# A gated-recurrence and GELU kernel: products of the identity on TensorE ahead of the first FFN matmul, and a smaller factor on the planned cost of the first attention steps

## The chip, the cores and the metric

One core of one Trainium2 chip (trn2) runs the kernel alone. The metric is the device time of one execution in microseconds; of several executions the median counts. The engines are called PE (TensorE), PEld (its weight loads), DVE (VectorE), ACT (ScalarE), POOL (GpSimd) and SP (SyncE, which issues most of the loads).

## The reference

The first half is a gated linear recurrence for 4 batches of 8 heads, 768 steps, head size 48; the second is a feed-forward layer (FFN) with GELU on its output, 3072 tokens by 384, with 2048 hidden columns. All of it is in float32.

```python
for t in range(S):
    state = alpha[:, :, t, :, None] * state + np.einsum('bhd,bhe->bhde', k[:, :, t], v[:, :, t])
    y[:, :, t] = np.einsum('bhd,bhde->bhe', q[:, :, t], state)
x = np.ascontiguousarray(y.transpose(0, 2, 1, 3)).reshape(B * S, H * D)
h = x @ w_in
g = 0.5 * h * (1.0 + erf(h * inv_sqrt2))
return (g @ w_out).astype(np.float32)
```

## The kernel before

**Attention.** The tokens are cut into 12 groups g of 256 steps. A group has two units (g, u), each four heads. For a unit, DVE makes running products of alpha forwards (`scan`, line 256), multiplies the queries by them (`qv`, line 261), makes them backwards and multiplies the keys (`back`, lines 265 and 268). PE forms the score products and transposes the keys (`scores`, lines 284 and 293) into one PSUM tile s. ACT copies the transposed keys out of it (`kn`, line 300) and DVE multiplies the scores by a mask (`mask`, line 305, output ss). Both read the same tile s, and the build orders them: the mask waits until kn is done. PE then multiplies by the values (`inside`, lines 322 and 340), DVE adds the states of the four chunks (`chain`, lines 357 and 359), PE adds what earlier states contribute (`outer`, line 384), and DVE hands the state on (`carry`, line 364).

**From attention to the FFN.** ACT copies the result as the high part of x (line 426). In the first three groups PE subtracts that part in PSUM (`x_minus`, line 435; its steps are called minus_x0, minus_x1, ...) and ACT copies the rest (line 441). After a group's second unit, small DMAs spread the last rows (line 449).

**FFN.** x and both weights are used as two float32r parts. There are 8 blocks f of 256 hidden columns. A step (g, f) is gemm1 (18 matmuls, line 457), two GELU passes on ACT (ghi and hp, lines 469 and 470), the low part glo (DVE, line 475; in the early steps by PE and ACT, lines 479 and 483), and gemm2 (12 matmuls, line 496) into two accumulators. When the next step belongs to another group, the accumulators are first copied out to a tile part (line 513 on ACT, 511 on DVE).

**Weights.** The 16 pieces of the weights (wi and wo of each f, in turn: piece 0 is wi of f = 0, piece 11 wo of f = 5) come as 64-bit words and are converted on the chip: u on ACT (line 183), c0 and c1 on DVE (lines 187 and 193, giving w), the high part on ACT (line 203: wih, woh), and four more on DVE (lines 206, 215, 224, 234), the last giving the low part (wil, wol). Until all eight f are there, only the first three groups are taken through the FFN.

**What sets the order.** A planner inside the kernel walks through time in steps of 0.05 us with a table of costs, lets each engine take the operation of lowest rank whose predecessors are done, and writes down a start for each. PE, DVE, ACT and SP then get their instructions in the order of these starts; each of them works through its queue in that order. The costs of `scores`, `inside` and `outer` of the first four units are multiplied by SLOW (1.8):

```python
if n < 4:
    for what in ("scores", "inside", "outer"):
        d[what].cost *= SLOW
```

At the very start PE multiplies the identity by itself 22 times (WARM, line 85); a float32 product is two passes on PE. PSUM tiles hp (of gemm1) come from a pool of two buffers.

Of the kernel before, what the change touches and what calls it, by code (L numbers as in the profile page):

```python
# [8 lines left out]
F32 = mybir.dt.float32  # L9
# [14 lines left out]
WARM = 22  # L24
XB = 3
WAIT = 0.15
SLOW = 1.8
UNTIL = 100.0
LANES = 8
RATE, ALONE, LATENCY, SMALL = 400e3, 290e3, 2.1, 50e3  # L30
# [10 lines left out]
def gla_then_gelu_ffn(ctx: ExitStack, tc: tile.TileContext, q, k, v, alpha, akq, w_in, w_out, out):  # L41
    nc = tc.nc
    B, H, D, S = q.shape
    NF, P, NK, _ = w_in.shape
# [3 lines left out]
    G = 2 * C  # L48
# [19 lines left out]
    ps_h = ctx.enter_context(tc.tile_pool(name="ps_h", bufs=2, space=PSUM))  # L68
    ps_o = ctx.enter_context(tc.tile_pool(name="ps_o", bufs=1, space=PSUM))

    ident = const.tile([P, P], F32, name="ident")
# [20 lines left out]
    minus = const.tile([P, P], F32R, name="minus")  # L92
# [551 lines left out]
    def plan_unit(n):  # L644
# [37 lines left out]
# [4 lines that stand above are left out]
# [47 lines left out]
    steps, plan, evacuated = [], [], set()  # L733
# [105 lines left out]
    def choose(e, t):  # L839
        best = None  # L840
        for o in waiting[e]:
            at = when(o)
            if at is not None and at <= t + 1e-9 and (best is None or (o.rank, o.n) < (best.rank, best.n)):
                best = o
        if e != "PE":
            return best
        if best is not None and not (best.late and best.at() + MARGIN > t):
            return best
        held = best
        second = [s for s in steps if s["gemm2"].start is None]  # L850
        if second:
            at = when(second[0]["gemm2"])
            if at is not None and at <= t + 1e-9:
                return second[0]["gemm2"]
        if len(second) < 2:
            hp_free = steps[-2]["low"].end if len(steps) > 1 else 0.0
            if hp_free is not None and hp_free + WAIT <= t + 1e-9 or len(steps) < 2:
                g = next_step(t)
                if g is not None:
                    return gemm1_op(g, t)  # L860
        return held
# [3 lines left out]
    while True:  # L865
        moved = False
        for e in ("DVE", "ACT", "PE", "SP", "POOL"):
            if free_at[e] <= t + 1e-9:
                o = choose(e, t)
# [12 lines left out]
    last["last"] = True  # L882
    plan.append(Op("DVE", "part", lambda: last["out"](), [last["gemm2"]]))
    plan[-1].start = t + 10
    plan.sort(key=lambda o: (o.start, o.n))

    by_hand = ExitStack()
# [71 lines left out]
```

## Time and profile before

| | |
|---|---|
| median of 3 runs | 534.9 us (534.61 to 537.7) |
| profiled execution | 533.34 us |
| its span, first to last instruction | 531.8 us |
| PE busy | 510.3 us (96%) |
| PEld busy | 492.8 us (93%) |
| DVE busy | 284.3 us (53%) |
| ACT busy | 207.8 us (39%) |
| mean granted clock of PE | 0.976 |

The busy shares are means over the span. In the kernel's first 80 us DVE is nearly full and PE isn't; later it is the other way round. A granted clock of 1.00 stands for 2.4 GHz, 0.50 for 1.2 GHz.

### The profile page before, as it was taken

What the parts mean: (1) busy time and instruction counts of PE and PEld (TensorE: products, weight loads), DVE (VectorE), ACT (ScalarE), POOL (GpSimd) and SP (SyncE); (2) the same over time, 40 slices, a digit from 0 to 9 for tenths busy, and PEclk for the clock granted to TensorE, in tenths of its full rate; (3) what the DMA queues carried; (4) which work ended last, traced back from release to release, by engine and by line L of the source; (5) the groups of instructions that cost most, each with busy time, mean ns of one, the idle gap of its engine ahead of it and who ended that gap; (6) DMA issues with size and microseconds to landing.
All of it is one profiled execution on the core that took longest, in us unless ns stands there. A gap on an engine that the chain in (4) does not pass through costs nothing.

```text
span 531.8 us, 13722 instructions
## 1 busy us (share of the span) xinstructions
PE 510.3 (96%) x5994; PEld 492.8 (93%) x5994; DVE 284.3 (53%) x543; ACT 207.8 (39%) x408; POOL 33.1 (6%) x45
## 2 busy tenths in 40 slices
PE   6689899989999999999999999999999999999995
PEld 6578889989999999999999999999999999999995
DVE  6999999998846655767565435242231121211211
ACT  2566766555433433444333333333222222222221
POOL 1000010000001100201010000000000000000000
PEclk9559999999999999999999999999999999999999
DMA  8856463422024323232242031000000000000001
GB/s 305 319 195 210 139 220 113 128 95 85 2 77 143 101 102 104 92 106 93 87 167 77 1 108 30 1 33 16 1 32 15 1 30 1 31 0 1 31 2 35
DMA packets 15249, 44.20 MB, mean 83 GB/s; under 512 B 2224, under 2 KB 5728, under 8 KB 15184
## 3 DMA queue, kind: packets, MB, share of 16 engines
q1 hardware_dynamic: 13520, 38.44, 22.0%
q0 software_dynamic: 1232, 4.33, 2.2%
q8 instruction: 49, 0.80, 0.6%
q10 hardware_dynamic: 432, 0.49, 0.3%
q14 instruction: 16, 0.13, 0.1%
HBM read 36.18 MB, written 4.72 MB: 77 GB/s over the span
## 4 chain that ended last, share of the span: by engine, by line
PE 83%; DVE 11%; issue 2%; DMA 1%; ACT 1%; SPq 0%; ACTq 0%; DVEq 0%
PE hp L457 36%; PE acc L496 35%; PE ybank L384 3%; PE ybank L322 2%; PE s L293 2%; PE s L284 2%; PE ybank L340 2%; DMA st<-in_moe_w_in_dram 1%; DVE w L193 1%; DVE st L224 1%; DVE u L187 1%; DVE pp L256 1%; DVE rp L265 1%; DVE state L359 1%; DVE u L206 1%
## 5 line engine op out<-in xcount | busy, mean ns | idle before, releaser
L457 PE MATMUL hp<-x,wih 128*128 128x256 f32 x1152 | 214.2, 286 | 0.0
L457 PEld LDWEIGHTS hp<-x,wih 128*128 128x128 f32 x1152 | 183.0, 192 | 1.5 <-PE acc L496 0.3
L457 PE MATMUL hp<-x,wil 128*128 128x256 f32 x576 | 163.4, 284 | 0.0
L475 DVE TENSOR_TENSOR glo<-hp,ghi 128x512 fp32r<-128x512 f32 x86 | 59.3, 690 | 173.4 <-ACT hp L470 172.6
L469 ACT ACTIVATE ghi<-hp 128x512 fp32r<-128x512 f32 x96 | 57.5, 599 | 227.8 <-PE hp L457 224.2
L496 PE MATMUL acc<-woh,ghi 128*128 128x384 f32 x384 | 130.9, 341 | 1.8 <-ACT part L513 1.8
L496 PE MATMUL acc<-wol,ghi 128*128 128x384 f32 x384 | 128.6, 335 | 0.0
L457 PEld LDWEIGHTS hp<-x,wil 128*128 128x128 f32 x576 | 110.8, 192 | 0.0
L496 PE MATMUL acc<-woh,glo 128*128 128x384 f32 x384 | 82.1, 334 | 0.0
L496 PEld LDWEIGHTS acc<-woh,ghi 128*128 128x128 f32 x384 | 72.4, 189 | 2.4 <-ACT part L513 2.0
L496 PEld LDWEIGHTS acc<-wol,ghi 128*128 128x128 f32 x384 | 72.5, 189 | 0.1
L496 PEld LDWEIGHTS acc<-woh,glo 128*128 128x128 f32 x384 | 68.0, 188 | 0.0
L470 ACT ACTIVATE hp<-hp 128x512 f32<-128x512 f32 x96 | 57.1, 595 | 0.0
L256 DVE TENSOR_TENSOR_SCAN pp<-akq,top 128x256 f32<-128x256 f32 x48 | 30.5, 677 | 31.1 <-DMA akq<-in_akq_dram 31.1
L261 POOL TENSOR_TENSOR akq<-akq,pp 128x512 f32<-128x512 f32 x18 | 23.3, 1293 | 212.0 <-DVE pe L257 172.3
L265 DVE TENSOR_TENSOR_SCAN rp<-akq,rp,top 128x255 f32<-128x255 f32 x48 | 34.6, 763 | 0.0
L384 PEld LDWEIGHTS ybank<-akq,state 48*48 48x48 f32 x704 | 22.2, 125 | 9.3 <-DVE state L359 5.1
L384 PE MATMUL ybank<-akq,state 48*48 48x64 f32 x704 | 25.9, 225 | 4.5 <-DVE state L359 4.5
L300 ACT COPY kn<-s 128x512 f32<-128x512 f32 x24 | 14.1, 587 | 38.8 <-PE ybank L340 33.6
L359 DVE TENSOR_TENSOR state<-ybank,state 128x96 f32<-128x96 f32 x80 | 20.5, 256 | 11.8 <-PE ybank L340 9.6
L521 POOL DMA_DIRECT2D out_dram<-part x11 | 8.3, 752 | 250.0 <-DVE part L515 197.0
L322 PEld LDWEIGHTS ybank<-ss,vn 64*64 64x64 f32 x768 | 14.2, 141 | 9.6 <-issue 3.2
(67 smaller groups left out, 401.8 us busy)
## 6 DMA issues: line engine op xcount, KB each, us to landing
akq<-in_akq_dram SPq DMA_DIRECT2D x22, 768.0 KB, 5.2
st<-in_moe_w_in_dram SPq DMA_DIRECT2D x8, 768.0 KB, 4.4
st<-in_moe_w_out_dram SPq DMA_DIRECT2D x8, 768.0 KB, 4.3
vn<-in_v_dram SPq DMA_DIRECT2D x12, 384.0 KB, 3.5
out_dram<-part POOLq DMA_DIRECT2D x11, 384.0 KB, 3.4
x<-z SPq DMA_DIRECT2D x63, 32.0 KB, 3.2
akq<-in_akq_dram SPq DMA_DIRECT2D x2, 512.0 KB, 4.9
akq<-in_akq_dram SPq DMA_DIRECT2D x2, 256.0 KB, 3.9
```

Source lines behind the costliest of these rows:

```text
L256: nc.vector.tensor_tensor_scan(pp[:, i], at[:, i], top, MID, ALU.mult, ALU.min)
L261: (nc.vector if g < NSB else nc.gpsimd).tensor_tensor(out=qt, in0=qt, in1=pp, op=ALU.mult)
L265: nc.vector.tensor_tensor_scan(rp[:, i, G - 2 :: -1], at[:, i, G - 1 : 0 : -1], top[:, 1:], rp[:, i, G - 1 :], ALU.mult, ALU.min)
L300: nc.scalar.copy(d["kn"], d["s"][:, :, 2 * C : 4 * C])
L322: nc.tensor.matmul(ybank[o, b, t : t + CS], lhsT=vn[r, c, e : e + DP], rhs=d["ss"][r, h, 2 * i + c, :], start=(i == 0 and c == 0), stop=(j ...
L359: d["chain"] = nc.vector.tensor_tensor(out=st[j + 1], in0=new, in1=st[j], op=ALU.add)
L384: ins = nc.tensor.matmul(ybank[r, b, t : t + CS], lhsT=states[u][j][r, i], rhs=d["qt"][r, i, j * CS : (j + 1) * CS], start=False, stop=Tru ...
L457: nc.tensor.matmul(hp[:, j, :], lhsT=a[:, j, i * P : (i + 1) * P], rhs=x[:, i, :], start=(j == 0 and i == 0 and n == 0), stop=(i == NK - 1 ...
L469: nc.scalar.activation(ghi, hp, AF.Gelu)
L470: nc.scalar.activation(hp, hp, AF.Gelu)
L475: nc.vector.tensor_tensor(out=glo, in0=hp, in1=ghi.bitcast(F32), op=ALU.subtract)
L496: nc.tensor.matmul(acc[t], lhsT=a[:, j, t * C : (t + 1) * C], rhs=w[:, j, :], start=(first and j == 0 and k == 0 and w is wo_hi[f]), stop= ...
```

## The change

SLOW goes from 1.8 to 1.2, so the planner reckons with shorter score, inside and outer steps in the first four units. When the plan is finished, a PSUM tile `spare` is taken from the pool of the hp tiles, and for each gap in PE's part of the plan ahead of its first gemm1 a number of identity products is put behind the step before the gap: as many as fit at 0.24 us each, with 0.3 us to spare. Nothing reads `spare`.

```diff
-SLOW = 1.8
+SLOW = 1.2
+FILL = 0.24
...
     plan[-1].start = t + 10
+    spare = ps_h.tile([P, 2, G], F32, tag="hp", name="spare")[:, 0, :P]
+
+    def busy(n):
+        for _ in range(n):
+            nc.tensor.matmul(spare, lhsT=ident, rhs=ident, start=True, stop=True)
+
+    first = min(o.start for o in plan if o.name == "gemm1")
+    early = sorted((o for o in plan if o.eng == "PE" and o.start <= first), key=lambda o: o.start)
+    for o, after in zip(early, early[1:]):
+        n = int((after.start - o.end - 0.3) / FILL)
+        if n > 0:
+            plan.append(Op("PE", "minus", lambda n=n: busy(n)))
+            plan[-1].start = o.start + 0.01
     plan.sort(key=lambda o: (o.start, o.n))
```

Lines 28 to 884 of before are one further down in the changed kernel; the identity products are its line 890. Besides the products, the new SLOW moves operations on all four planned engines. Three places matter here. In the names, s_0_1, ss_0_1, kn_0_1 belong to unit (0, 1); hp_0_3, ghi_0_3 and glo_0_3 to step (0, 3); the last number is a buffer's.

DVE, from the queries of unit (0, 1) on. Before:

```order
L261 TENSOR_TENSOR akq0_118<-akq0_118,pp_0_1_203 128x512
L265 SCALAR_TENSOR_TENSOR rp_0_1_204<-akq0_118,rp_0_1_204,top_114 128x255 x2
L268 TENSOR_TENSOR akq0_118<-akq0_118,rp_0_1_204 128x512
L305 TENSOR_TENSOR ss_0_0_239<-s_0_0_210,mask_133 128x512
L187 TENSOR_SCALAR u_0_231<-u_0_231 128x768
L193 SCALAR_TENSOR_TENSOR w_0_276<-st_0_183,u_0_231 128x768
```

Now:

```order
L262 TENSOR_TENSOR akq0_118<-akq0_118,pp_0_1_204 128x512
L306 TENSOR_TENSOR ss_0_0_242<-s_0_0_211,mask_133 128x512
L266 SCALAR_TENSOR_TENSOR rp_0_1_205<-akq0_118,rp_0_1_205,top_114 128x255 x2
L269 TENSOR_TENSOR akq0_118<-akq0_118,rp_0_1_205 128x512
L358 COPY state0_1_124<-ybank_137 128x96
```

The mask of unit (0, 0) has moved ahead of back(0, 1), and chain(0, 0) ahead of the first conversion. The mask still waits for kn(0, 0), which on ACT stands second, behind u of piece 0, in both kernels.

PE, from minus_x0 of unit (0, 1) to the first gemm1. Before:

```order
L435 MATMUL ybank_137<-z0_414,minus_104 128x128 x2
L435 MATMUL ybank_137<-x0_338,minus_104 128x128 x2
L284 MATMUL s_1_0_424<-akq1_120 64x64 x16
L293 MATMUL s_1_0_424<-ident_76,akq1_120 128x128 x4
L322 MATMUL ybank_137<-ss_1_0_457,vn1_119 64x64 x16
L340 MATMUL ybank_137<-vn1_119,kn_1_0_459 64x48 x16
L457 MATMUL hp_0_0_510<-x0_338,wih0_138 128x256 x2
```

Now:

```order
L890 MATMUL spare_176<-ident_76 128x128 x2
L436 MATMUL ybank_137<-z0_424,minus_104 128x128 x2
L436 MATMUL ybank_137<-x0_337,minus_104 128x128 x2
L890 MATMUL spare_176<-ident_76 128x128 x19
L285 MATMUL s_1_0_474<-akq1_120 64x64 x16
L294 MATMUL s_1_0_474<-ident_76,akq1_120 128x128 x4
L458 MATMUL hp_0_0_498<-x0_337,wih0_138 128x256 x2
```

19 identity products stand between the two, and gemm1 of step (0, 0) has moved ahead of inside(1, 0). The other 23 products are behind scores(0,0) (5), inside(0,0) (1), outer(0,0) (5), the first minus_x0 (3), inside(0,1) (7) and outer(0,1) (2). The order of the FFN steps among themselves is the same in both kernels.

ACT, from the second GELU pass of step (0, 3) on. Before:

```order
L470 ACTIVATE hp_0_3_1508<-hp_0_3_1508 128x512
L203 CAST woh5_159<-w_11_1557 128x768
L513 COPY part2_175<-acc0_2_0_1316 128x384
L513 COPY part2_175<-acc1_2_0_1317 128x384
L469 ACTIVATE ghi_0_4_1601<-hp_0_4_1562 128x512
```

Now:

```order
L471 ACTIVATE hp_0_3_1552<-hp_0_3_1552 128x512
L514 COPY part2_175<-acc0_2_0_1355 128x384
L514 COPY part2_175<-acc1_2_0_1356 128x384
L204 CAST woh5_159<-w_11_1600 128x768
L470 ACTIVATE ghi_0_4_1643<-hp_0_4_1602 128x512
```

The copies of the accumulators of group 2 have moved ahead of the high part of piece 11. Two further moves lie just ahead of this place: on ACT, u of piece 11 now stands before ghi(0, 3), and on DVE glo(2, 4) before the low part wil5.

## Rows read from the trace of the kernel before

**Rows 1.** The page: the granted clock of PE in 40 slices of 13.3 us, in tenths of full speed.

```profile
PEclk9559999999999999999999999999999999999999
```

**Rows 2.** Stretches of the span, from:to in us and their length; busy time of PE, PEld, DVE, ACT and POOL with instruction counts, PE's granted clock, mean share of the DMA engines, GB/s.

```profile
14.50:38.20 23.70, 17.16 (x282) 15.02 (x274) 23.01 (x48) 12.67 (x23) 0.00 (x0) 0.50 0.76 267
38.20:60.00 21.80, 19.30 (x363) 17.06 (x363) 20.77 (x41) 14.61 (x30) 0.00 (x0) 1.00 0.57 184
...
80.00:112.40 32.40, 32.40 (x359) 31.22 (x359) 31.61 (x51) 18.61 (x35) 3.89 (x3) 1.00 0.37 122
...
117.20:526.00 408.80, 408.77 (x4588) 399.33 (x4586) 174.97 (x347) 140.38 (x281) 25.09 (x24) 1.00 0.16 52
```

**Rows 3.** PE alone in half-microsecond stretches: length, busy time and instructions, granted clock, DMA share, GB/s. The two stretches in which the clock changes.

```profile
14.00:14.50 0.50, 0.50 (x46) 0.91 1.07 430
...
38.00:38.50 0.50, 0.50 (x7) 0.70 0.00 0
```

**Rows 4.** The warm-up passes (line 85) in two short looks at the timeline, late in the warm-up: start, time from the first start to the last end, and the passes that this covers.

```profile
8.01 0.50 PE L85 MATMUL warm<-ident 128*128 128x128 f32 x3
...
8.23 0.39 PE L85 MATMUL warm<-ident 128*128 128x128 f32 x2
```

**Rows 5.** PE's timeline: start, time from the first start to the last end, instructions, and in brackets the idle time before and what ended it. In order: the first products of inside(0,0), of scores(1,0) and of inside(1,0), the first and the last matmul of gemm1(0,0), outer(2,0), and the first products of scores(2,1).

```profile
13.45 0.69 PE L322 MATMUL ybank<-ss,vn 64*64 64x64 f32 x32 [2.48 <-DVE ss L305]
...
29.06 1.13 PE L284 MATMUL s<-akq 48*64 48x64 f32 x32
...
32.35 1.13 PE L322 MATMUL ybank<-ss,vn 64*64 64x64 f32 x32 [1.12 <-issue]
...
34.29 0.79 PE L457 MATMUL hp<-x,wih 128*128 128x256 f32 x2
...
38.09 0.38 PE L457 MATMUL hp<-x,wil 128*128 128x256 f32 x1
...
56.17 1.10 PE L384 MATMUL ybank<-akq,state 48*48 48x64 f32 x32 [1.35 <-DVE state L359]
...
62.17 0.69 PE L284 MATMUL s<-akq 48*64 48x64 f32 x32
```

**Rows 6.** DVE's timeline, columns as above: qv(0,1), back(0,1) (two rows), mask(0,0), c0 of piece 0, three of the four sums of chain(0,0), the scans of unit (1,0), the last product of back(1,0), that of back(2,1), and wil5.

```profile
9.70 0.67 DVE L261 TENSOR_TENSOR akq<-akq,pp 128x512 f32<-128x512 f32 x1
...
10.29 1.38 DVE L265 TENSOR_TENSOR_SCAN rp<-akq,rp,top 128x255 f32<-128x255 f32 x2
11.71 0.69 DVE L268 TENSOR_TENSOR akq<-akq,rp 128x512 f32<-128x512 f32 x1
12.70 0.69 DVE L305 TENSOR_TENSOR ss<-s,mask 128x512 f32<-128x512 f32 x1 [0.30 <-ACT kn L300]
13.31 0.55 DVE L187 TENSOR_SCALAR u<-u 128x768 int32<-128x768 int32 x1
...
16.98 0.84 DVE L359 TENSOR_TENSOR state<-ybank,state 128x96 f32<-128x96 f32 x3
...
19.21 1.26 DVE L256 TENSOR_TENSOR_SCAN pp<-akq,top 128x256 f32<-128x256 f32 x2
...
28.27 0.69 DVE L268 TENSOR_TENSOR akq<-akq,rp 128x512 f32<-128x512 f32 x1
...
59.62 0.69 DVE L268 TENSOR_TENSOR akq<-akq,rp 128x512 f32<-128x512 f32 x1
...
107.78 0.96 DVE L234 SCALAR_TENSOR_TENSOR wil<-st,u 128x768 fp32r<-128x768 f32 x1
```

**Rows 7.** ACT's timeline, its first two operations: u of piece 0 and kn(0,0).

```profile
11.23 0.89 ACT L183 ACTIVATE u<-st 128x768 f32<-128x768 f32 x1 [9.01 <-DMA st<-in_moe_w_in_dram]
12.02 0.57 ACT L300 COPY kn<-s 128x512 f32<-128x512 f32 x1
```

**Rows 8.** Waits by pair of lines: us in total, times, longest. DVE from 12 to 115 us (two of its three rows), and PE from 60 to 110 us (its one row).

```profile
DVE ss L305 <- ACT kn L300: 0.7, 2, 0.4
DVE ss L305 <- PE s L293: 0.7, 1, 0.7
...
PE hp L479 <- ACT hp L470: 0.7, 1, 0.7
```

**Rows 9.** A row of the chain of work that ended last (start, length, what): gemm1(2,0) at 79.77 us, behind gemm2(1,2). Then the timelines of PE, ACT and DVE around 113 us: the last matmul of gemm1(0,4), the first of gemm2(0,3); the two GELU passes of step (0,3), woh5 and the copies of part2; c1 of piece 11 (w) and glo(0,3).

```profile
79.77 2.35 PE hp L457 x18
...
112.67 0.28 PE L457 MATMUL hp<-x,wil 128*128 128x256 f32 x1
114.76 0.44 PE L496 MATMUL acc<-woh,ghi 128*128 128x384 f32 x1 [1.81 <-ACT part L513]
...
109.58 0.58 ACT L469 ACTIVATE ghi<-hp 128x512 fp32r<-128x512 f32 x1
110.06 0.59 ACT L470 ACTIVATE hp<-hp 128x512 f32<-128x512 f32 x1
...
113.49 0.83 ACT L203 CAST woh<-w 128x768 fp32r<-128x768 f32 x1 [2.84 <-DVE w L193]
114.23 0.86 ACT L513 COPY part<-acc 128x384 f32<-128x384 f32 x2
...
112.50 0.96 DVE L193 SCALAR_TENSOR_TENSOR w<-st,u 128x768 int32<-128x768 int32 x1
113.38 0.68 DVE L475 TENSOR_TENSOR glo<-hp,ghi 128x512 fp32r<-128x512 f32 x1
```

## The prediction

> **What bounds the kernel now.** I read the page first, then the stretches of the span, the clock in half-microsecond steps, the timelines of TensorE, VectorE and ScalarE from 9 to 40 us, the waits, and last the chain around 80 and 113 us. The page's clock row shows one dip, in the second and third of 40 slices [rows 1]. By stretches the span falls into three parts [rows 2]. From 14.5 to 38.2 us PE is busy for 17.16 of 23.70 us at half clock, while DVE is busy for 23.01: there VectorE is the bound, and PE waits for it and for ScalarE in short pieces. From 38.2 to 60 it has 19.30 of 21.80 us, from 80 on 32.40 of 32.40, then there is one hole of 1.81 us at 113 [rows 9], and then it has 408.77 of 408.80. So a gain at 30 us reaches the end only if it is still there at 80 us and again behind the hole.
>
> The clock falls during 14.0 to 14.5 us, after TensorE had stood still for 2.48 us ahead of inside(0,0) [rows 3, 5], and comes back at about 38.2 us, when TensorE has worked from 32.35 us on without a break.
>
> **The fillers.** 42 products of the identity are added in seven places: 5, 1, 5, 3, 7, 2 and 19. Each is two passes, and two passes are 0.22 us at full clock [rows 4], so 0.44 at half: 9.2 us in all, or 18.5. At full clock they lie in time in which TensorE waited anyway, and cost nothing; the cover is gone if the clock is low when the row of 19 starts. That row stands between minus_x0 (over at about 26.9 us by a walk through the queues with these durations) and scores(1,0), which can't start before about 31.4 (below): 4.2 us of filler at full clock fit, 8.4 at half clock would end 3.9 us too late.
>
> **What full clock is worth.** The same steps at both levels: the score products 1.13 us against 0.69; gemm1 takes from 34.29 to 38.47, 4.18 us, against 2.35 [rows 5, 9]. That is a ratio of 0.56 to 0.61, so the 17.16 busy us at half clock hold about 7.2 us of excess. This is the ceiling, not the gain: VectorE had only 0.7 us free in that stretch [rows 2]. The Trainium skill (TensorE: Matmul & The Clock Gate, section "What's actually happening") puts the cost of a kernel's slow ramp below 1% of a typical span, which here would be 5.3 us; the dip of this trace holds 7.2, or 1.35%. By the page a gain of over 1% would be out of reach, by the rows just within it; both lie above what I take, and the row goes into the chances.
>
> **What the new order adds to VectorE.** With SLOW at 1.2 the planner believes in quicker score, inside and outer steps and moves mask(0,0) ahead of back(0,1). But mask(0,0) waits on ScalarE: in the trace it starts 0.30 us late, released by kn(0,0) (line 300), which stands behind u_0 (line 183), and that waits for the first weight to land, 11.23 us; kn ends at 12.59 [rows 6, 7]. Nothing of this moves, since the loads ahead of it are the same. VectorE now arrives at the mask at 10.37 (end of line 261) instead of 12.40, and stands there until 12.70: a wait of 2.33 us for one of 0.30. Back(0,1), 2.1 us of scans and product, is queued behind it; behind that come chain(0,0), c0 of piece 0 and the whole conversion chain. Then back(0,1) ends at 12.70 + 0.6 + 2.1 = 15.4, scores(0,1) at 16.65 (0.69 for the products and about as much for the transposes), kn(0,1) 0.57 later at 17.25, while VectorE is through chain (1.1, of which 0.84 for three of its four sums) and c0 (0.5) at 17.0: some 0.35 us more on the second mask. So **VectorE runs about 2.4 us later** than before from the scans of unit (1,0) on, which began at 19.21 [rows 6]. It has nothing to catch up with until waits of its own fall away: after the first 0.30 these were 0.4 and 0.7 us up to 115 us [rows 8], so the lag at 113 us is about 1.3.
>
> **Where the two meet.** Scores(1,0) follows back(1,0), which ended at 28.96: now 31.4. Scores to 32.7, gemm1(0,0) at full clock to 35.1, inside(1,0) to 36.2 (1.1, as its 1.94 from 32.35 to 34.29 were at half clock); before, the same three were done at 38.47. TensorE is 2.2 us ahead although VectorE is 2.4 behind. But every later attention step follows VectorE, and TensorE takes its queue in order: scores(2,1) began at 62.17, 1.86 us after its back(2,1) was done (60.31) [rows 5, 6]. With the lag that is 62.7, 0.5 us later: the lead is spent. On to 79.77, where through gemm2(1,2) and scores(3,0) both orders have done the same steps, a wait of 0.65 us for the GELU (line 479) is the only loss of before [rows 8]; in the new order scores(3,0) stands behind gemm2(1,2), where its back has had the time, and that wait has other work to lie beside. So 0.5 - 0.65 = -0.15 us at 80 us. The bounds: the whole lag, +2.4, and -2.0 if the wait of 1.35 us for line 359 that it had at 56 us [rows 5] goes as well.
>
> **The hole at 113.** gemm2(0,3) was ready at 112.95 and began at 114.76, 1.81 us late, released by the copies of part2 (line 513) [rows 9]. These stood on ScalarE behind woh5 (line 203), which waited for VectorE's w at 113.46. In the new order the copies stand ahead of woh5. They don't come free at once: u_11 has moved ahead of ghi(0,3), and it waits for wil5 on VectorE, which ended at 108.7 [rows 6] and now, with 1.3 of lag and glo(2,4) moved ahead of it (0.7), ends at about 110.7; u_11 (0.9), two GELU passes (1.1) and the copies (0.86) end at about 113.5. gemm2(0,3) starts there, and its second half waits for glo(0,3), which started at 113.38 [rows 9] and now ends at about 115.4. It is over at about 116.1 instead of 117.11. Of that I take 0.7 us as the gain, with 0 (the lag eats it) and 1.81 as the ends.
>
> **The sum.** -0.15 - 0.7 = -0.85 us, against 533.34 us of the profiled execution, whose span is 531.8: 532.5. That execution was 1.56 us under the median of the three runs (534.9), so the forecast for the median is 534.05, in round terms **534.1 us**. After 117 us TensorE works through to the end, with the same steps, and nothing there changes.
>
> **Rivals.** (1) *VectorE's wait goes through to the end.* The mechanism is the 2.33 us at mask(0,0). It decides when an attention step, not an FFN step, is the last thing TensorE waits for before 80 us, and the hole at 113 grows by what is left of the lag instead of shrinking. For it speaks that VectorE is 97% busy from 14.5 to 38.2 us, and that TensorE's waits there are for it; against it, 7.2 us of cheaper matmuls in the same queue, and 1.86 us of slack at 62 us. Price: up to +2.4, so 537.3. (2) *The clock isn't held.* The fillers are sized by a plan that does not know of the wait at mask(0,0): with the five of the first place used up at 12.0, TensorE stands still until about 13.45, 1.4 us, and again for 0.8 before scores(0,1) and 1.6 before outer(0,1). A hole of 1.35 us at 56 us left the clock alone, one of 2.48 did not; between them no row speaks. If it falls at 14.4, inside(0,1) and the fillers behind it take twice as long and the chain on VectorE waits some 1.5 us more; the 7 and the 19 fillers would then keep TensorE working long enough to bring the clock back, as from 32.35 to 38.2, so the 3.9 us hardly come on top. Price: +1.5 to +3.5, 536.4 to 538.4. (3) *More than I take is kept:* the whole hole at 113 and 0.65 us before it, -2.5: 532.4.
>
> **How the numbers follow.** Forecast (533.3 to 535.3) 0.45; rival 1, 0.25; rival 2, 0.12; rival 3, 0.18. The range from 532.2 to 537.6 takes in rivals 1 and 3, the lower half of rival 2, and the ends of the terms; it leaves out gains above 2.7 us and a lag with a lost clock on top. One per cent, 5.3 us, is about what a measurement of this kernel can tell from no change. To be faster by that, three quarters of the excess would have to pass a VectorE that is full: 0.02. To be slower by it, rivals 1 and 2 would have to add up: 0.04. Within 1%: 0.94.
>
> **What would show it.** Right: the granted clock stays at 1.00 from 15 to 38 us; ss at line 306 has a wait of over 2 us on kn at about 10.4 us; the scans of unit (1,0) start near 22.0 instead of 19.21; gemm1(0,0) ends at about 35; at about 80 us both kernels have done the same steps; the wait of gemm2(0,3) at 113 us is under 1.2 us. Wrong: the clock at 0.50 after 14.5 us; a wait of TensorE for VectorE of over 2 us between 40 and 80 us; or mask(0,0) without its wait, which would put the time near rival 3 or below.

## The result, and the profile after

The changed kernel takes **537.62 us** (median of 20 executions, 534.92 to 540.56), the kernel before 534.75 (20 executions, 533.22 to 537.7): a ratio of 1.0051, 95% interval 1.0034 to 1.0067. It is slower by half a per cent, where a gain of 0.15% was forecast. The profiled execution took 537.89 us with a span of 536.3, against 533.34 and 531.8 before; since that one of before was a quick one, the spans differ by 4.5 us and the medians by 2.9.

The page's clock row, and the stretches that answer to [rows 1, 2] (length, busy time of PE, PEld, DVE, ACT, POOL with counts, granted clock, DMA share, GB/s):

```profile
PEclk9999899999999999999999999999999999999998
...
14.50:38.20 23.70, 18.96 (x349) 17.30 (x348) 22.56 (x45) 12.42 (x23) 0.00 (x0) 1.00 0.71 236
38.20:60.00 21.80, 17.21 (x260) 15.42 (x261) 19.92 (x39) 13.26 (x27) 0.00 (x0) 0.89 0.54 170
...
80.00:112.40 32.40, 30.88 (x363) 28.94 (x364) 31.62 (x52) 20.07 (x38) 3.85 (x3) 1.00 0.40 132
112.40:117.20 4.80, 4.80 (x37) 4.80 (x36) 4.72 (x9) 2.23 (x4) 0.01 (x1) 1.00 0.17 27
```

The clock is held up to 38 us, and the hole at 113 us [rows 9] is gone. But from 38 to 60 us PE is busy for 2.1 us less than before, at a clock of 0.89.

DVE's timeline (start, length, operation, in brackets the idle time and what ended it), to be held against [rows 6]: both masks of group 0, the scans of unit (1,0), carry(1,0), chain(2,0), mask(2,1), and the low part of piece 11, called wol5 below.

```profile
12.59 0.69 DVE L306 TENSOR_TENSOR ss<-s,mask 128x512 f32<-128x512 f32 x1 [2.29 <-ACT kn L301]
...
17.34 0.69 DVE L306 TENSOR_TENSOR ss<-s,mask 128x512 f32<-128x512 f32 x1 [0.52 <-ACT kn L301]
...
21.78 1.27 DVE L257 TENSOR_TENSOR_SCAN pp<-akq,top 128x256 f32<-128x256 f32 x2
...
42.76 0.26 DVE L365 SCALAR_TENSOR_TENSOR state<-state,pe 128x96 f32<-128x96 f32 x1 [0.98 <-PE ybank L385]
...
63.15 0.84 DVE L360 TENSOR_TENSOR state<-ybank,state 128x96 f32<-128x96 f32 x3 [2.35 <-PE ybank L341]
...
68.43 0.69 DVE L306 TENSOR_TENSOR ss<-s,mask 128x512 f32<-128x512 f32 x1 [0.95 <-ACT kn L301]
...
122.33 0.96 DVE L235 SCALAR_TENSOR_TENSOR wol<-st,u 128x768 fp32r<-128x768 f32 x1
```

Before, DVE came to wol5 at

```profile
115.90 0.96 DVE L234 SCALAR_TENSOR_TENSOR wol<-st,u 128x768 fp32r<-128x768 f32 x1
```

The low parts of the 16 pieces come on DVE in the same order in both kernels, so their starts tell its lag: 2.6 us at piece 1 (27.97 against 25.38), 2.4 at piece 2, 3.8 at piece 3, 3.3 at piece 4, 6.7 at piece 5, 6.4 at piece 11. Each large step up stands behind waits: 2.29 and 0.52; 0.98 at 42.76 and one of 0.38 at 44.87; 2.35 and 0.95 at 63 and 68 us. In between the lag changes by less than 1 us.

Where these waits come from, on PE's timeline: the rest of gelu(0,0), and the first matmul of gemm1(1,0). With them the granted clock in the stretches behind, and what ACT did ahead of the first:

```profile
38.00 0.80 PE L480 MATMUL hp<-ghi,minus 128*128 128x512 f32 x1 [1.78 <-ACT hp L471]
...
58.12 0.52 PE L458 MATMUL hp<-x,wih 128*128 128x256 f32 x2 [2.80 <-DMA x<-z]
...
38.00:41.30 3.30, 3.30 (x10) 3.20 (x11) 3.16 (x9) 2.06 (x4) 0.00 (x0) 0.50 0.59 218
...
58.10:61.80 3.70, 3.68 (x18) 3.65 (x18) 2.64 (x6) 0.93 (x1) 0.00 (x0) 0.55 0.50 172
...
35.57 1.28 ACT L470 ACT_TABLE_LOAD   x1
36.86 0.60 ACT L470 ACTIVATE ghi<-hp 128x512 fp32r<-128x512 f32 x1
```

At 38 us PE has waited 1.78 us for the first GELU, which stands behind a table load of 1.28 us. At 58.12 us it has waited 2.80 us for the small copies of x1. After both pauses the clock is at half (1.2 GHz): gemm2(0,0) goes at 0.32 us a matmul, and gemm1(1,0) takes 3.92 us where 2.35 would do. In the new order inside(2,0) stands behind gemm1(1,0), so it comes at 62.0 us, and DVE's chain(2,0) waits for it. Before, inside(2,0) and outer(2,0) stood ahead of gemm1(1,0), and the copies had been there in time.

The issues of these copies, first before, then after (queue, count, size, median us to landing), and SP's queue around them (start, length):

```profile
x<-z SPq DMA_DIRECT2D x3, 32.0 KB, 2.0
x<-z ACTq DMA_DIRECT2D x3, 32.0 KB, 2.3
...
48.56 0.34 SPq L139 DMA_DIRECT2D akq<-in_akq_dram  x1
52.15 1.78 SPq L449 DMA_DIRECT2D x<-z  x3
```

```profile
x<-z SPq DMA_DIRECT2D x3, 32.0 KB, 5.3
x<-z ACTq DMA_DIRECT2D x3, 32.0 KB, 5.4
...
48.39 0.37 SPq L173 DMA_DIRECT2D st<-in_moe_w_in_dram  x1
50.63 0.34 SPq L140 DMA_DIRECT2D akq<-in_akq_dram  x1
52.40 1.78 SPq L450 DMA_DIRECT2D x<-z  x3
```

The copies go out at the same time, but the 768 KB load ahead of them now leaves 1.8 us before them instead of 3.6, and the weight piece (44.56 us before) at 48.39. The copies lie beside both and take 3 us more. That load is released by outer(1,1), which the lag has put at 49.5 us (47.4 before).

Where the delay stands can be read at a step that both kernels have, scores(2,1) on PE. Its products now, and every wait that the timeline shows for PE behind them up to 121 us:

```profile
66.55 0.63 PE L285 MATMUL s<-akq 48*64 48x64 f32 x30
...
80.37 0.50 PE L480 MATMUL hp<-ghi,minus 128*128 128x512 f32 x1 [0.55 <-ACT hp L471]
...
87.88 0.47 PE L458 MATMUL hp<-x,wih 128*128 128x256 f32 x2 [0.91 <-DMA x<-z]
...
120.55 0.96 PE L497 MATMUL acc<-woh,glo 128*128 128x384 f32 x4 [0.17 <-DVE glo L476]
```

Before, these products began at 62.17 us [rows 5]. From there to the end of the span it is 469.6 us before and 469.8 now, so all but 0.1 us of the loss is there by 67 us. It is 4.4 us: gemm1(1,0) begins 0.9 us later (58.12 against 57.20), takes 1.6 more at half clock, and inside(2,0) and outer(2,0), together 2.0 us, come behind it instead of ahead of it; smaller moves take 0.1 off.

Last, the end of the chain of waits (start, length, what), before and after:

```profile
112.50 0.97 DVE w L193
...
114.23 0.48 ACT part L513
...
114.76 2.35 PE acc L496 x12
117.11 2.15 PE hp L457 x18
```

```profile
117.28 1.64 DVE u L188
...
119.81 0.69 DVE glo L476
...
120.55 0.96 PE acc L497 x4
121.51 2.16 PE hp L458 x18
```

In both kernels the chain comes over DVE's conversions and then stays on PE to the end. That alone doesn't make DVE's queue the cause. mask(2,1) at 68.43 us waited for kn(2,1), which follows PE's scores(2,1). From there DVE works 51.4 us up to glo(0,3) without a wait, and PE, which comes to the same point by its own queue, waits only 0.17 us for it. **From 67 us on both queues are full and carry the same delay.** The low part wol5 is a place to read it, not the place where it arises.

The hole at 113 us is gone, and yet nothing is gained there: from the start of scores(2,1) to the end of gemm2(0,3) it was 54.94 us (62.17 to 117.11) and is 54.96 (66.55 to 121.51). DVE's stretch from mask(2,1) to glo(0,3) has grown from 49.8 to 51.4 us; three conversion steps of piece 5 (lines 207, 216 and 225, 1.9 us together) now stand behind mask(2,1).

### The profile page after: what moved, and what is told of

Its sections match the earlier page's. It is cut to its first block, busy times and chain, and to the rows that moved or that the text cites. A ratio compares the mean times of both kernels' runs of the same rounds, so it can differ in the third digit from the quotient of the medians.

```text
span 536.3 us, 13885 instructions
## 1 busy us (share of the span) xinstructions
PE 516.2 (96%) x6078; PEld 499.3 (93%) x6078; DVE 285.0 (53%) x543; ACT 208.1 (39%) x408; POOL 33.0 (6%) x45
## 4 chain that ended last, share of the span: by engine, by line
PE 80%; DVE 11%; DMA 3%; issue 2%; ACT 2%; SPq 0%; DVEq 0%
PE hp L458 35%; PE acc L497 34%; PE ybank L385 4%; PE ybank L323 2%; PE s L294 2%; DMA x<-z 2%; PE s L285 2%; PE ybank L341 2%; DMA st<-in_moe_w_in_dram 1%; DVE pp L257 1%; DVE u L188 1%; DVE st L225 1%; DVE w L194 1%; DVE rp L266 1%; DVE u L207 1%
## 5 line engine op out<-in xcount | busy, mean ns | idle before, releaser
L385 PEld LDWEIGHTS ybank<-akq,state 48*48 48x48 f32 x704 | 21.0, 120 | 6.1 <-DVE state L360 1.9
L385 PE MATMUL ybank<-akq,state 48*48 48x64 f32 x704 | 24.6, 219 | 1.5 <-DVE state L360 1.5
L184 ACT ACTIVATE u<-st 128x768 f32<-128x768 f32 x16 | 14.5, 908 | 26.6 <-DVE wol L235 9.8
```

What stands on the lines that cost most here:

```text
L184: nc.scalar.activation(d["u"], staged[n].bitcast(F32)[:, 1::2], AF.Copy, scale=2.0**-112)
L385: ins = nc.tensor.matmul(ybank[r, b, t : t + CS], lhsT=states[u][j][r, i], rhs=d["qt"][r, i, j * CS : (j + 1) * CS], start=False, stop=Tru ...
```

## Experiments

Four theories stood against each other: A, the copies of x1 (and the clock that falls in the pause); B, DVE's lag from mask(0,0); C, the products themselves; later D, DVE's queue as what gathers all of it. Ratios are against the kernel before.

| kernel | median us | ratio, 95% interval | wol5 on DVE, us | span of that execution |
|---|---|---|---|---|
| after | 537.62 | 1.0051 (1.0034 to 1.0067) | 122.33 | 536.3 |
| order_only | 537.97 | 1.0056 (1.0035 to 1.0077) | 120.80 | 534.5 |
| fill_only | 534.85 | 0.9995 (0.9968 to 1.0022) | 117.59 | 533.2 |
| inside_first | 536.78 | 1.0026 (1.0009 to 1.0044) | 122.79 | 536.7 |
| fill_on | 535.87 | 1.0012 (0.9991 to 1.0032) | 120.75 | 534.5 |
| loads_behind | 535.78 | 1.0022 (1.0005 to 1.0040) | 119.29 | 533.0 |
| back_first | 536.95 | 1.0034 (1.0013 to 1.0056) | 121.89 | 536.1 |
| dve_old | 536.67 | 1.0029 (1.0004 to 1.0055) | 119.25 | 533.5 |
| kn_first | 534.50 | 0.9991 (0.9968 to 1.0014) | 117.39 | 531.4 |
| loads_back | 536.28 | 1.0022 (0.9997 to 1.0048) | 119.01 | 532.9 |
| loads_fill | 535.19 | 1.0006 (0.9983 to 1.0029) | 119.69 | 533.7 |
| loads_back_fill | 534.02 | 0.9991 (0.9969 to 1.0014) | 118.59 | 532.4 |
| dve_loads | 535.43 | 1.0012 (0.9986 to 1.0039) | 117.61 | 531.7 |
| dve_loads_fill | 534.87 | 0.9991 (0.9966 to 1.0016) | 119.52 | 533.3 |
| kn_fill | 534.81 | 1.0005 (0.9987 to 1.0024) | 119.83 | 533.6 |
| **kn_loads_fill** | **532.41** | **0.9965 (0.9946 to 0.9984)** | 116.35 | 530.2 |
| fill_all | 534.47 | 0.9998 (0.9977 to 1.0020) | 116.20 | 531.8 |
| part_first | 533.71 | 0.9977 (0.9960 to 0.9994) | 117.58 | 532.7 |
| fill_all_part | 534.14 | 0.9975 (0.9957 to 0.9994) | 117.56 | 532.8 |

The last two columns are of one execution each, and executions of one kernel differ by 2 to 7 us, so they are to be read with each other and not with the median. In the 15 kernels with the new order the span is 413.7 to 414.3 us longer than the start of wol5, while that start itself moves by 6.4 us. In before it is 415.9.

Counted from PE's start of scores(2,1), the rest of the span is 469.5 to 470.0 us in the 15, while that start moves from 60.53 us (kn_loads_fill) to 67.00 (inside_first); in before it is 469.6. In all 15, mask(2,1) waits 0.6 to 2.9 us for kn(2,1), DVE then works 51.4 us to glo(0,3) without a wait, and PE stands there for 0.18 us at most. So D holds as a reading: a lag at wol5 is a lag of the end. As a cause it isn't shown, because PE sets DVE's lag anew at mask(2,1). What the kernels differ in lies ahead of that.

### Order or products

order_only is the kernel before with the new factor and nothing else, so it has no products. fill_only is the changed kernel with the old factor:

```diff
-SLOW = 1.8                                                           # order_only, against before
+SLOW = 1.2
...
-SLOW = 1.2                                                           # fill_only, against after
+SLOW = 1.8
```

> The planner's new order (the factor 1.2) without any of the 42 products. Theory A (what costs is the new place of gemm1(1,0): ahead of inside(2,0) it waits 2.8 us for the copies of x1, which land beside two 768 KB loads, and the pause drops the clock again): the wait stays, 2 to 3 us at 58 us, and the clock is low before 38 us as well, so 537 to 539 us. Theory B (DVE's mask(0,0) waits 2.3 us for kn(0,0) and DVE stays late to the end): the same wait, 537.6 us. Theory C (the products themselves get in the way of PE): 534.8 us, the time of the kernel before.

order_only measured 537.97 us. In its trace gemm1(1,0) waits 0.80 us for the copies and not 2 to 3, but it begins at 58.01 us, as after: PE comes later to the same landing.

> The products, counted from the same rule, in the order of the kernel before (factor 1.8). Theory A: inside(2,0) and outer(2,0) stand ahead of gemm1(1,0) again, no wait for the copies of x1, 534.0 to 535.0 us; the clock at 1.00 up to 38 us is worth under 1 us. Theory B: mask(0,0) stands behind back(0,1) on DVE again, no wait, 534.8 us too. Theory C: 537.6 us, as after.

fill_only measured 534.85 us. The order alone costs all of it, the products cost nothing: C has fallen. The clock from 14.5 to 38.2 us (0.54 in order_only, 1.00 after) is worth 0.35 us of the median, which can't be told from nothing.

### The pause at 58 us

inside_first puts inside(2,0) ahead of gemm1(1,0); fill_on puts products into the pauses at 36 and 55 us; loads_behind moves the copies ahead of the two loads on SP.

```diff
+    gemms[1, 0].start = unit[4]["inside"].start + 0.005              # inside_first
...
+            for _ in range(11): nc.tensor.matmul(hp[:, 0, :P], lhsT=ident, rhs=ident, ...)   # fill_on, in gemm1(1, 0)
...
+    plan.append(Op("PE", "minus", lambda: busy(7)))                  # fill_on
+    plan[-1].start = unit[2]["inside"].start + 0.01
...
+    for i, o in enumerate((wops[6]["get"], unit[7]["load"])):        # loads_behind
+        o.start = ready_x[1][0].start + 0.01 + 0.01 * i
```

> The changed kernel with one step moved: inside(2,0) ahead of gemm1(1,0) on PE, as it stands in the kernel before; all else, the products and DVE's early order among it, as after. Theory A: PE works in the 2.8 us pause, gemm1(1,0) starts when the copies have landed (58.1 us) at a full clock and takes 2.35 us, not 3.92, and DVE's chain(2,0) is 4 to 5 us earlier: 534.5 to 536.0 us. Theory B: 537.6 us, since DVE's wait at 10 us is still there.

inside_first measured 536.78 us. inside(2,0) now has PE for itself, but starts no earlier than gemm1 did (PE's timeline):

```profile
58.77 0.69 PE L323 MATMUL ybank<-ss,vn 64*64 64x64 f32 x32 [2.50 <-DVE ss L306]
```

The pause is about as long, for DVE this time: mask(2,0) is late by the lag. (In this execution the clock was at 0.50 from 15.5 to 22 us, and the lag at piece 2 is 3.4 us where after has 2.4.) A in its first form, with the copies as the one cause, has fallen.

> The changed kernel with 18 more products: 7 ahead of the rest of gelu(0,0) (the 1.78 us pause at 36.2 us) and 11 ahead of gemm1(1,0) (the 2.80 us pause at 55.3 us). Order and waits as after. Theory A, the clock's share of it: the granted clock stays at 1.00 at 38 to 41 and 58 to 62 us, gemm2(0,0) is some 1.4 us and gemm1(1,0) some 1.6 us shorter, the wait for the copies of x1 stays at 2.8 us: 535.0 to 536.3 us. Theory B: 537.6 us. If the wait alone matters and the clock's loss is made up later: 537 to 537.6 us.

fill_on measured 535.87 us. The wait for the copies is gone with it, since the products reach as far as their landing.

> The changed kernel with SP's copies of x1 moved ahead of the weight piece and of the loads of unit (3,1) that stand before them; nothing else. Theory A: the copies land in 2 to 3 us instead of 5.3, gemm1(1,0) starts at 55.3 us and not at 58.1 with the clock still full (2.35 us, not 3.92), inside(2,0) follows it: 533.8 to 535.5 us. Theory B (DVE is late): gemm1(1,0) starts early but the same pause comes one step later, ahead of inside(2,0), which waits for DVE's mask(2,0): 536.5 to 537.6 us.

loads_behind measured 535.78 us, between the ranges of A and B. Each of the two gets back 1.8 us of the median. In fill_on the clock is full from 55.7 to 62 us, but fell in another pause (0.69 from 43.7 to 47.5 us). In loads_behind the copies land in 2.2 to 2.9 us by the median, but gemm1(1,0) waits 1.80 us for the last of them and begins at 57.30. SP issues the weight piece 0.1 us behind them; that this holds the last one up is not shown.

### DVE's first stretch

```diff
+    unit[1]["back"].start = unit[0]["mask"].start - 0.01             # back_first
...
+    row = [unit[1]["back"], unit[0]["mask"]] + [wops[0][k] for k in ("c0", "c1", "c2", "c3", "c4")]   # dve_old
+    for i, o in enumerate(row):
+        o.start = 10.26 + 0.01 * i
+    for i, o in enumerate((unit[0]["chain"], wops[0]["lo"])):
+        o.start = 13.0 + 0.01 * i
+    unit[2]["scan"].start = unit[1]["mask"].start + 0.01
...
+    unit[0]["kn"].start = wops[0]["u"].start - 0.01                  # kn_first
```

> The changed kernel with one step moved: on DVE back(0,1) ahead of mask(0,0), as it stands in the kernel before. DVE then works where it waited 2.3 us for kn(0,0), and its steps from scan(1,0) on are some 2 us earlier (19.8 instead of 21.8 us). Theory B (this wait goes through to the end): 535.0 to 535.7 us. Theory A (the copies of x1 behind two large loads set gemm1(1,0), and the clock falls in the pause): outer(1,1), the loads and the copies move forward together, the pause ahead of gemm1(1,0) stays at 2 to 3 us, PE gains 1 to 2 us up to there: 535.5 to 536.8 us. Neither matters: 537.6 us.

back_first measured 536.95 us. The wait wasn't taken away. DVE's timeline, mask(0,0), chain(0,0) and mask(0,1):

```profile
13.09 0.69 DVE L306 TENSOR_TENSOR ss<-s,mask 128x512 f32<-128x512 f32 x1 [0.81 <-ACT kn L301]
15.08 0.26 DVE L358 COPY state<-ybank 128x96 f32<-128x96 f32 x1 [1.30 <-PE ybank L341]
...
17.31 0.69 DVE L306 TENSOR_TENSOR ss<-s,mask 128x512 f32<-128x512 f32 x1 [0.63 <-ACT kn L301]
```

The one wait of 2.29 us has become three, of 2.7 together, and the scans of unit (1,0) start at 21.75 us. So it doesn't test B.

> The changed kernel with DVE's first stretch as before: back(0,1), mask(0,0), then c0 to c4 of piece 0, and only then chain(0,0), the low part, mask(0,1) and the scans of unit (1,0). The conversion then fills the time in which DVE waited (2.29 and 0.52 us). Theory D (DVE's queue sets the end: its lag at the low part of piece 11 goes over into the span one for one): the lag of 2.4 us at the scans falls to under 1, some 2 us of the 2.9 come back: 535.0 to 536.0 us. Theory A (the copies of x1 and the clock at 58 us are all): 537 us or more.

dve_old measured 536.67 us. The first piece's low part is early (17.99 us), but DVE then waits 1.3 us for PE ahead of a chain, and 1.6 to 1.8 us of lag are back at pieces 1 and 2. Under 1 us of the median is gained.

> The changed kernel with ACT's kn(0,0) ahead of u of piece 0, so that it no longer stands behind the landing of the first weight; DVE's new order stays. mask(0,0) then starts at 11.3 to 11.6 instead of 12.59 us, inside(0,0) and chain(0,0) with it; the scans of unit (1,0) some 1 us earlier (20.8). Theory D: 536.3 to 537.0 us. If the wait only moves on to chain(0,0) or to mask(0,1): 537.6 us.

kn_first measured 534.50 us. That is 3.1 us less than after, all of the change's loss, by one step on ACT: the forecast for D (0.6 to 1.3) was far too small. ACT's and DVE's timelines:

```profile
9.73 0.59 ACT L301 COPY kn<-s 128x512 f32<-128x512 f32 x1 [7.51 <-PE s L294]
...
10.42 0.69 DVE L306 TENSOR_TENSOR ss<-s,mask 128x512 f32<-128x512 f32 x1 [0.28 <-ACT kn L301]
...
19.61 1.27 DVE L257 TENSOR_TENSOR_SCAN pp<-akq,top 128x256 f32<-128x256 f32 x2
...
117.39 0.96 DVE L235 SCALAR_TENSOR_TENSOR wol<-st,u 128x768 fp32r<-128x768 f32 x1
```

The lag is 0.3 us at piece 2 and 1.5 at piece 11. Mask, inside and chain all come 2.2 us earlier, so nothing takes the wait over. The load of unit (3,1) goes out at 48.60 us again, the copies of x1 at 50.37, land in 3.7 us, and gemm1(1,0) waits 0.87 and 0.33 us for them instead of 2.80. scores(2,1) begins at 61.63 us, 4.9 earlier. More than half of the pause at 58 us was itself a consequence of the wait at 10 us.

### Copies, clock and lag together

These join the edits above; 12 products are 7 ahead of the rest of gelu(0,0) and 5 ahead of inside(1,1). Where an expectation speaks of the former, it is for loads_back loads_behind and back_first, for loads_back_fill loads_back, for dve_loads dve_old, for dve_loads_fill dve_loads, and for kn_loads_fill kn_fill.

```diff
+    for o, n in ((unit[2]["inside"], 7), (unit[2]["xm"], 5)):
+        plan.append(Op("PE", "minus", lambda n=n: busy(n)))
+        plan[-1].start = o.start + 0.01
```

> Both of the former edits at once (copies of x1 ahead of the loads, back(0,1) ahead of mask(0,0)). If both the copies and DVE's lag can each set PE's pause at 55 us, only this one removes it: 533.0 to 534.5 us, less than either edit alone by 1 us or more. If one of them is the cause alone, the time is that of its single edit.

loads_back measured 536.28 us.

> As the former, with 12 more products: 7 ahead of the rest of gelu(0,0) (pause of 1.8 us) and 5 ahead of inside(1,1) (1.25 us). If the clock falls in one of these pauses, the granted clock over 38 to 60 us goes from some 0.9 to 0.97 or more and the time is 1 us less than the former: 532 to 533.5 us. If the clock's loss is made up by waits behind it: no difference.

loads_back_fill measured 534.02 us.

> The changed kernel with SP's copies of x1 ahead of the two loads and the 12 further products of loads_back_fill, but with DVE in its new order (mask(0,0) ahead of back(0,1), waiting 2.3 us for kn(0,0)). If DVE's lag has a share of its own in the 2.9 us: 534.8 to 536 us, some 1 us above loads_back_fill (534.0). If copies and clock are all of it: 533.7 to 534.4 us.

loads_fill measured 535.19 us.

> As the former, with SP's copies of x1 ahead of the two loads. Theory D: the lags add up, DVE's low part of piece 11 at 116.5 to 117.5 us instead of 122.3, 533.0 to 534.3 us. Theory A: as with the copies moved alone, 535.8 us.

dve_loads measured 535.43 us.

> As the former, with 12 more products ahead of the rest of gelu(0,0) and of inside(1,1). Theory D: some 0.5 to 1 us less than the former by the clock: 532.3 to 533.6 us, below the kernel before. Theory A: 534.0 us, as without DVE's old order.

dve_loads_fill measured 534.87 us.

> The changed kernel with kn(0,0) ahead of u of piece 0 on ACT and 12 more products ahead of the rest of gelu(0,0) and of inside(1,1). If the clock's falls behind 38 us still cost something there: granted clock 0.996 or more, 533.0 to 534.0 us. If DVE alone sets the time: 534.5 us as with kn moved alone.

kn_fill measured 534.81 us.

> As the former, with SP's copies of x1 ahead of the two loads as well. Theory D (what is left of the 2.9 us is DVE's lag, clock and copies each put in their part): 532.0 to 533.3 us, below the kernel before by 1.5 to 2.5. If the copies no longer matter with DVE early: as the former.

kn_loads_fill measured 532.41 us.

loads_back, dve_loads and dve_loads_fill came out 1 to 2 us above what was expected: since back_first and dve_old don't take the lag away, they add little to loads_behind. A late DVE can still hold PE up where the copies are quick: in loads_back and dve_loads PE waits 1.01 us for back(2,1) ahead of scores(2,1). Of the clock the pairs say different things: 12 products more gave 2.3 us (loads_back), 0.6 (loads_behind, dve_loads) and nothing (kn_first, 0.3 slower), and in each pair the intervals overlap. The copies count even with DVE early: kn_loads_fill is 2.4 us below kn_fill, where in the profiled execution they took 5.1 us and gemm1(1,0) waited 2.03 and 0.97. In kn_loads_fill they take 2.0 to 2.2 us by the median (gemm1(1,0) still waits 1.57 for the last), the clock doesn't fall in the profiled execution, and wol5 is 0.45 us behind before:

```profile
PEclk9999999999999999999999999999999999999998
...
116.35 0.96 DVE L235 SCALAR_TENSOR_TENSOR wol<-st,u 128x768 fp32r<-128x768 f32 x1
```

With 532.41 us it beats both kernels, before by 0.16 to 0.54%. So two causes stand side by side: what mask(0,0) waits for (3.1 us when removed alone) and the copies of x1 behind the loads (1.8 alone, with intervals that overlap; 2.4 with the first removed and the 12 products in). With 12 products they make 5.2 us together; no kernel has both without these products. Both act ahead of scores(2,1), which kn_loads_fill begins at 60.53 us.

### The order of before, made better

```diff
+    next(s["evac"] for s in steps if s["g"] == 2 and s.get("evac")).start = wops[11]["hi"].start - 0.01   # part_first
```

```diff
+    more = [(unit[0]["inside"], 5, busy), (unit[0]["outer"], 8, busy), (unit[2]["inside"], 4, busy), (gemms[0, 0], 6, busy)]   # fill_all
+    more += [(unit[3]["outer"], 2, busy_ahead), (unit[4]["scores"], 5, busy_ahead), (unit[4]["outer"], 4, busy_ahead)]
+    for o, n, fill in more:
+        plan.append(Op("PE", "minus", lambda n=n, fill=fill: fill(n)))
+        plan[-1].start = o.start - 0.005
```

busy_ahead writes into the tile that gemm1(1,0) is to use. fill_all and fill_all_part have the factor 1.8, as fill_only.

> The kernel before, without products, with one step moved: ACT's two copies of the third group's partial sum ahead of the conversion woh5, behind which they stand and on which PE waits 1.81 us at 113 us. If ACT's order alone makes that pause: 533.0 to 534.0 us. If DVE (busy 4.73 of the 4.80 us there) is late right behind it, PE waits for DVE instead: 534.3 to 534.8 us.

part_first measured 533.71 us.

> The order of the kernel before, with the products of the rule and 34 more in the pauses of over 0.5 us that are left up to 58 us (ahead of inside(0,0), outer(0,0), inside(1,0), gemm1(0,0), outer(1,1), scores(2,0) and outer(2,0)). If the clock's falls are what spreads the executions and costs time: granted clock 0.996 or more, 533.0 to 534.2 us, and executions within 2 us of one another. If the waits, which the products don't touch, set the time: 534.5 to 535.0 us as without the 34.

fill_all measured 534.47 us.

> Both of the former edits: 1 to 2 us below the one with all the products, 531.5 to 533.0 us, if the two gains are independent; the same as it, if PE then waits for DVE behind 113 us.

fill_all_part measured 534.14 us.

fill_all holds the clock at 1.00 throughout in its profiled execution; by the median of its executions it has 0.993, before 0.973. It gains 0.4 us of the median, which can't be told from nothing: in this order the clock ahead of 58 us isn't shown to be worth anything. fill_all_part is no faster than part_first: the two gains don't add up. part_first gains 1.2 of the 1.81 us, and then PE stands behind DVE (PE's waits from 105 to 130 us: lines, sum, times, longest):

```profile
PE acc L496 <- DVE glo L475: 0.9, 1, 0.9
```

## Why the prediction was wrong

**The fillers: right in the profiled execution.** There they held the clock from 15 to 38 us, and they cost nothing (fill_only). The 7.2 us of excess were indeed a ceiling with next to nothing under it: order_only and the changed kernel differ by 0.35 us, or 0.07%. The Trainium skill's rule (TensorE: Matmul & The Clock Gate, "What's actually happening") that the ramp penalty is below 1% of a typical span agrees with that.

**VectorE's first stretch: right.** A wait of 2.33 us was worked out, 2.29 came; the second mask 0.35 against 0.52; the scans of unit (1,0) at 22.0 against 21.78. gemm1(0,0) ended at 35.1 as said.

**"Where the two meet": the step that failed.** The working had scores(2,1) at 62.7 us, 0.5 later than before, and PE 0.15 us ahead at 80 us. It began at 66.55, 4.4 us later, and at the checkpoint the same steps were done 4.4 us later (84.2 against 79.77). That is the whole loss, and more than the term's upper bound of +2.4. The lead of PE was followed to inside(1,0) at 36.2 us, and the next steps were taken from the old trace. Two waits stood at nothing without a reason. The rest of gelu(0,0) was not looked up: its GELU has the table load ahead of it, which before lay beside the slow gemm1(0,0), on an ACT that idled 1.89 us behind it. (The Trainium skill, ScalarE: Activation LUTs, "What ACT_TABLE_LOAD costs", gives 1.283 us for the load and 1.38 for a drain with it; the row has 1.28, and the GELU starts 0.01 us behind it, so the trace shows no drain.) And gemm1(1,0), which the new order puts ahead of inside(2,0), was not asked for its copies, for which PE waited 2.80 us. Nor was a second fall of the clock reckoned with: it fell in both new pauses.

**The hole at 113 us: a gain of 0.7 that came to nothing.** PE's stall there did go, as the working had it, and gemm2(0,3) did wait for glo(0,3), over at 115.4 us in the working and at 120.5 in the trace. But from scores(2,1) on the new order takes 469.8 us, against 469.6. The 1.3 us of lag in that term were 6.4 at wol5. Subtracting DVE's old waits of 0.4 and 0.7 was right: neither is in the trace of the changed kernel. What was missing are the waits that DVE got from PE and from kn at 42.76, 44.87, 63.15 and 68.43 us, 4.7 in all: 2.4 - 1.1 + 4.7 is 6.0 of the 6.4.

**Rivals.** The first named the right wait: kn_first, which removes what mask(0,0) waits for and nothing else, gives back 3.1 us. That its price (537.3) is near the time is partly luck. It took the wait itself as the most that could be lost, and an attention step as what PE would wait for last; PE's last long wait was for the copies ahead of an FFN step. In its favour stood that DVE was busy for 31.61 of 32.40 us from 80 to 112 us [rows 2], when PE was full too; the working read that row of PE alone. The second, a clock that falls before 38 us, did not come in the profiled execution. It did in that of inside_first, which has the same order and products up to there: after a pause of 2.42 us ahead of inside(0,0) the clock was at 0.50 from 15.5 to 22 us. Of the signs for being right, all came but the one at 80 us; of those for being wrong none, for the clock fell at 38 us and not behind 14.5. The sign at 80 us was the one that counted.

**Open.** How much the clock's fall at 38 and 58 us costs by itself: the pairs give 0 to 2.3 us, none of them clear. By their intervals inside_first, loads_behind, back_first and dve_old are not clear of the changed kernel; fill_on, kn_first and kn_loads_fill are. (The intervals reach some 0.2% to either side, or 1 us, where the prediction took 5.3 us as what can be told from no change.)

## What to carry to other kernels

Where one engine is full up to the point at which the bound passes to another, a wait on it need not be absorbed: follow its lag at a step that recurs (here the low part of each weight piece), and expect the lag to grow where it delays a step that it will itself wait for. Then follow the other engine too, and look for a step from which the rest takes equally long in both kernels (here scores(2,1)): the loss lies ahead of it, however late the chain of waits shows another engine. Before moving the waiting step, look at what releases it: one copy moved ahead of an operation that waits for a load gave back as much as the reordering had cost. A step that moves ahead needs its small transfers too, at the time and beside the loads of the new order.

## What the runs showed of the hardware

- How soon copies of 32 KB land goes with the loads of 768 KB around them (medians of SP's copies): 2.0 us with the last load issued 3.6 us ahead (before), 3.7 with one 1.8 us ahead (kn_first), 5.3 with two, 1.8 and 4.0 us ahead (after). In loads_behind and kn_loads_fill the loads are issued 0.1 us behind SP's last copy; the medians are 2.9 and 2.0, and PE still waits 1.80 and 1.57 us for the last copy.
- The granted clock was at half after pauses of PE of 2.80 and 1.78 us in the changed kernel, 2.42 and 2.50 in inside_first, and 1.25 in fill_on. It stayed full over 1.41 and 1.25 in the changed kernel, 1.35 before [rows 5], 2.02 and 1.80 in loads_behind and 2.05 in dve_old. The length of a pause alone doesn't tell.
- Executions of one kernel differ by their mean granted clock: after, 540.56 us at 0.982, 536.42 to 537.94 at 0.990, 534.92 at 0.996 (correlation of the 20: -0.79; in loads_back -0.97, from 539.6 at 0.983 to 533.1 at 0.997). A single execution can be 3 us from its kernel's median.
